# Linear-attention denominators by DMA transpose and VectorE instead of a TensorE matmul

## The chip, the cores and the metric

The kernel runs on one core of one Trainium2 chip. The metric is the device time of one execution in microseconds (us). A core has five engines that run their own instruction streams side by side and meet at semaphores: TensorE (PE in the profile; its weight loads are listed as PEld), VectorE (DVE), ScalarE (ACT), GpSimd (POOL) and SyncE (SP), which here only issues DMAs. SP issues them one after the other: where the next DMA waits for a semaphore, all that are behind it in the program wait too.

## The reference

Two linear-attention blocks A and B with weights of their own run on the same x (2048 rows, 640 columns), and a sigmoid gate mixes them. Each has 32 heads of 20 columns.

```python
def block(x, wqkv, wo):                          # A and B alike
    q, k, v = split(x @ wqkv)                    # 32 heads of 20 columns
    phi = lambda t: where(t > 0, t + 1, exp(t)) + 1e-6
    pq, pk = phi(q), phi(k)
    kv  = einsum("bhsd,bhse->bhde", pk, v)
    z   = einsum("bhsd->bhd", pk)                # column sums of pk
    num = einsum("bhqd,bhde->bhqe", pq, kv)
    den = einsum("bhqd,bhd->bhq", pq, z) + 1e-6  # one number for each row of x and head
    return (num / den) @ wo

g = sigmoid((x * gate_w).sum(-1))
out = g * block_A(x) + (1 - g) * block_B(x)
```

The change concerns `den`, its inverse, and how the inverse, times the gate, comes to the values of pq that it scales.

## The kernel before

The 2048 rows are 16 tiles of 128 (`t`) or four blocks of 512 (`b`). The 640 columns of q and k are five groups `g` of 128: group g holds the columns g, g+5, g+10 and so on, so a partition p of any group belongs to head p // 4, and each head has four neighbouring partitions, 4h to 4h+3.

The order of the work on PE is the order in which the program text makes it. On the other engines a planner in the kernel (`Sched`) lays every instruction into a timeline by an assumed cost and a priority; the program that results is fixed, and each engine runs its instructions in that order. The stages on PE are:

- K for A and B (L513, L514), from the start to 48 us; exp on ACT, min and add on DVE, results in PKA and PKB.
- G of A (L644, L645), pk transposed times x, with a column of ones that yields z; between its matmuls the query units (`q_unit`, L767): five matmuls fill one PSUM bank, ACT takes exp (L784) and relu (L791) of it, DVE puts them together as pq (L794, L802), in EX, PKA or GSA.
- G of B with the rest of the query units, and between them for A: kv (`kv_unit`, L685, masked by DVE at L700), the denominators (`den`, L850), and WP = kv times wo (`wp_unit`, L721, copied by ACT at L735 and moved into place by DMA).
- The outputs of A for 13 tiles (`o_part`, L937, kept by ACT), and between them the denominators, kv and WP of B; then the outputs of B for these tiles (`o_rest`, added by DVE at L974), then three tiles with A and B in one accumulation.

The results of G leave PSUM by ACT (L653) into WKW, and a DMA transpose of 128x640 turns them into GSA and GSB.

The denominators go as follows. `t_sum` (L827, L830) multiplies pq of each group by its z, a scalar for each partition, and adds the five groups in float32; the last addition writes bf16 into TSH, 128 x 512 for each block. `den` multiplies a 128x32 mask of ones (the columns of CST from 24 on) with TSH: four matmuls put the four blocks into 32 partitions each of one PSUM bank, so that partition 32b+h holds the denominators of head h in block b. ACT adds 1e-6 (L869), DVE inverts (L879, eight RECIPROCALs of 128x128 for A and B together) and multiplies by the gate (L888). The gate, known for each row of x as a column, had been turned by DVE (L610), written to DRAM by four DMAs and read back by eight that spread it over 32 partitions. Nine DMAs copy each row of the product to the four partitions of its head (FXT: for A over WVA, for B over XN), and DVE multiplies pq by it in halves of 256 rows (`pqs`, L915). `o_mm` (L937) waits for the half it reads and for WP.

Of the kernel before, what the change touches and what calls it, by code (L numbers as in the profile page):

```python
# [28 lines left out]
def _consts():  # L29
    p = np.arange(128)[:, None]  # L30
    bd = (p // 20 == np.arange(24)[None, :] // 4).astype(np.float32)
    zm = (p // 4 == np.arange(H)[None, :]).astype(np.float32)
    return _bf16_bits(np.concatenate([bd, zm], axis=1))


CW = 24 + H
XS_W = 672
KB_W = 648

# [219 lines left out]
def body(nc, A_x, A_wqkv, A_wo, B_x, B_wqkv, B_wo, gate_w, out, log=None):  # L259
# [53 lines left out]
    TSF = [TSB[:, 1024 * b : 1024 * b + 1024].bitcast(f32) for b in range(NB)]  # L313
    TSH = sb("TSH", [128, NB, 512], bf)
    ZC = sb("ZC", [128, 2 * NC], f32)
    DTT = sb("DTT", [128, 512], f32)
    RCT = sb("RCT", [128, 512], f32)
    FF = {X: sb("FF" + X, [128, 512], bf) for X in XS}
    GB = {X: sb("GB" + X, [128, 512], f32) for X in XS}
    CST = sb("CST", [128, CW], bf)  # L320
    GW5 = sb("GW5", [NC, 128], bf)
    GE = sb("GE", [128, NT], f32)
    GG = sb("GG", [128, 2, NT], f32)
    GT = sb("GT", [128, 32], f32)
    ONE = sb("ONE", [128, 128], bf)
    SCR = sb("SCR", [128, 1], f32)
    EPSC = sb("EPSC", [128, 1], f32)
    PS = nc.alloc_psum_tensor("ps", [128, 8, 512], f32)

    GD = nc.dram_tensor("ggd", [2, S], f32, kind="Internal").ap()  # L330

    IDN = sb("IDN", [128, 128], bf)
    BDM = CST[0:GR, 0:24]
    ZMK = CST[:, 24:CW]

    sch = Sched({"ps": 8, "ek": NEK, "eq": NEQ, "os": NOS})
    op = sch.op
# [257 lines left out]

    LOW = 10**6

    bge2, bgg, bgg2, bgt = Buf("ge2"), Buf("gg"), Buf("gg2"), Buf("gt")
    op("DVE", lambda e: e.tensor_scalar(GG[:, 1, :], GE[:, :], 1.0, None, op0=ALU.add), 150.0, ins=bge, outs=[bge2], prio=LOW + 50, name="ge1")
    op("DVE", lambda e: e.reciprocal(GG[:, 0, :], GG[:, 1, :]), 250.0, ins=[bge2], outs=[bgg], prio=LOW + 51, name="gr")  # L600
    op(
# [5 lines left out]
        prio=LOW + 52,  # L607
        name="gm",
    )
    op("DVE", lambda e: e.transpose(GT[:, :], GG[:, :, :].rearrange("p a b -> p (a b)")), 200.0, ins=[bgg, bgg2], outs=[bgt], prio=LOW + 53, name="gt")  # L610
    bgd = []
    gflat = GD.rearrange("a (t q j) -> (a t) q j", q=4, j=32)
    for q in range(4):
        b = Buf("gd%d" % q)
        bgd.append(b)
        dma("SP", "gd%d" % q, gflat[:, q, :], GT[32 * q : 32 * q + 32, :], 4096, ins=[bgt], outs=[b])
    bgb = {X: [] for X in XS}
    for i, X in enumerate(XS):
        for j in range(NB):
            b = Buf("gb")  # L620
            bgb[X].append(b)
            dma(
                "SP",
                "gb%s%d" % (X, j),
                GB[X][32 * j : 32 * j + 32, :],
                GD[i, 512 * j : 512 * j + 512].partition_broadcast(32),
                65536,
                ins=bgd,
                outs=[b],
            )  # L630


    bgs = {}
    bz = {}
# [37 lines left out]
        )  # L672

    bkvl = {X: [] for X in XS}

    def kv_unit(X):
        gv = GS[X][:, :, :].rearrange("p c (g m) -> p c g m", g=NC)
        for us in ((0, 1, 2, 3), (4, 5)):
            ps = Buf("kv", "ps")

            def fn(e, us=us, ps=ps):
                for i, u in enumerate(us):
                    lo = GR * u if u < 5 else D - GR
                    for c in range(NC):
                        r = e.matmul(  # L685
                            PS[0:GR, ps.slot, GR * i : GR * i + GR],
                            WV[X][:, c, lo : lo + GR],
                            gv[:, c, :, lo // 5 : lo // 5 + 24],
                            start=(c == 0),
                            stop=(c == NC - 1),  # L690
                        )
                return r

            op("PE", fn, 5 * len(us) * mm_cost(GR), ins=[bwv[X]] + [bgs[X, g] for g in range(NC)], outs=[ps], name="kv" + X)
            b = Buf("kvl")
            bkvl[X].append(b)
            n = len(us)
            op(
                "DVE",
                lambda e, us=us, ps=ps, n=n: e.tensor_tensor(  # L700
                    out=KVL[X][:, us[0] : us[0] + n, :].rearrange("p u (m g) -> p u g m", g=NC),
                    in0=PS[0:GR, ps.slot, 0 : GR * n].rearrange("p (u g m) -> p u g m", u=n, g=NC),
                    in1=BDM.unsqueeze(1).unsqueeze(1).to_broadcast([GR, n, NC, 24]),
                    op=ALU.mult,
                ),
                dve1(GR * n),
                ins=[ps, bcst],
                outs=[b],
                prio=-1,
                name="kvm",  # L710
            )
# [99 lines left out]
    def scale_now(X, b, h):  # L811
        pqs_op[X, b, h].prio = len(sch.ops)

    prev_rc = [[], []]

    bts, last_ts = {}, {}

    def t_sum(X, b):
# [3 lines left out]
        for g in range(NC):  # L822
# [1 line left out]
            src = PQ[X, b][:, g, :]  # L824
            n = Buf("ts")
            if g == 0:
                f = lambda e, z=z, src=src: e.tensor_scalar(TSF[b], src, z, None, op0=ALU.mult)  # L827
            else:
                dst = TSF[b] if g < NC - 1 else TSH[:, b, :]
                f = lambda e, z=z, src=src, dst=dst: e.scalar_tensor_tensor(dst, src, z, TSF[b], op0=ALU.mult, op1=ALU.add)  # L830
# [1 line left out]
            if b in last_ts and g == 0:  # L832
                after = [last_ts[b]]
            if g == NC - 1 and X == "B":
                after = [den_op["A"]]
            last = op(
                "DVE", f, dve1(512), ins=[bz[X, g], bpq[X, b, g]] + prev, outs=[n], after=after, prio=LOW + 20 * i + b, name="ts"
            )
# [1 line left out]
        last_ts[b] = last  # L840
        bts[X, b] = n

    den_op = {}

    def den(X):
        ps = Buf("den", "ps")

        def fn(e):
            for j in range(NB):
                r = e.matmul(  # L850
                    PS[32 * j : 32 * j + 32, ps.slot, :],
                    ZMK,
                    TSH[:, j, :],
                    start=True,
                    stop=True,
                    tile_position=(0, 32 * j),
                )
            return r

        den_op[X] = op("PE", fn, mm_cost(512) + 200, ins=[bcst] + [bts[X, b] for b in range(NB)], outs=[ps], name="den" + X)  # L860
        dops = [sch.ops[-1]]
        halves = []
        for h in range(2):
            q = slice(256 * h, 256 * h + 256)
            b1, b2, b3 = Buf("dt"), Buf("rc"), Buf("ff")
            halves.append(b3)
            op(
                "ACT",
                lambda e, q=q: e.activation(DTT[:, q], PS[:, ps.slot, q], ACT.Identity, bias=EPSC[:, 0:1], scale=1.0),  # L869
                act_cost(256),  # L870
                ins=[ps, beps],
                outs=[b1],
                after=prev_rc[h][0:1],
                name="dt",
            )
            for k in (256 * h, 256 * h + 128):
                rc = op(
                    "DVE",
                    lambda e, k=k: e.reciprocal(RCT[:, k : k + 128], DTT[:, k : k + 128]),  # L879
                    1010.0,  # L880
                    ins=[b1],
                    outs=[b2],
                    after=prev_rc[h][1:2],
                    name="rc",
                )
            ff = op(
                "DVE",
                lambda e, q=q: e.tensor_tensor(out=FF[X][:, q], in0=RCT[:, q], in1=GB[X][:, q], op=ALU.mult),  # L888
                dve1(256),
                ins=[b2] + bgb[X],  # L890
                outs=[b3],
                name="ff",
            )
            prev_rc[h] = [rc, ff]
        for b in range(NB):
            parts = ((0,), (1,)) if X == "B" and b == 0 else ((0, 1),)
            for hs in parts:
                bx = Buf("fx")
                q = slice(256 * hs[0], 256 * hs[-1] + 256)
                dma(  # L900
                    "SP",
                    "fx%s%d%d" % (X, b, hs[0]),
                    FXT[X][:, b, q],
                    FF[X][32 * b : 32 * b + 32, q].unsqueeze(1).to_broadcast([H, 4, 256 * len(hs)]),
                    65536 * len(hs),
                    ins=[halves[h] for h in hs],
                    outs=[bx],
                    issue=650.0,
                )
                for h in hs:  # L910
                    bs = Buf("pqs")
                    bfx[X, b, h] = bs
                    pqs_op[X, b, h] = op(
                        "DVE",
                        lambda e, b=b, h=h: e.tensor_tensor(  # L915
                            out=PQ[X, b][:, :, 256 * h : 256 * h + 256],
                            in0=PQ[X, b][:, :, 256 * h : 256 * h + 256],
                            in1=FXT[X][:, b, 256 * h : 256 * h + 256].unsqueeze(1).to_broadcast([128, NC, 256]),
                            op=ALU.mult,
                        ),  # L920
                        150 + 1280 * 0.52,
                        ins=[bx] + [bpq[X, b, g] for g in range(NC)],
                        outs=[bs],
                        after=dops,
                        name="pqs",
                    )


    def o_mm(X, t, ps, lo, hi, first="A", last="B"):
# [185 lines left out]
```

## Time and profile before

| | |
|---|---|
| median of 5 runs | 189.73 us (189.42 to 190.11) |
| the profiled execution | 189.42 us |
| its span, first to last instruction | 188.0 us |
| VectorE busy | 128.7 us |
| ScalarE busy | 95.9 us |
| denominator matmuls L850 | 8, each recorded with 390 ns, at 105.1 us (A) and 142.7 us (B) |
| DTT activations L869 | 4, median 476 ns |
| RECIPROCAL L879 | 8, mean 920 ns |
| gate multiplication L888 | 4 of 128x256, 425 to 494 ns |
| pqs L915 | 16 of 128x1280, mean about 820 ns |
| copies FFA to WVA and FFB to XN | 9 DMAs, about 2.6 us from issue to landing |
| mean granted TensorE clock | 1.000 |

A busy time is the time in which the engine had an instruction of its own in work. TensorE's matmuls overlap: a 128x512 matmul is recorded with some 380 ns, but in a run of them a new one starts about every 216 ns. So what a matmul costs the engine is read from the distance of the starts. In a group's line, the idle time behind the bar is that of the engine just before these instructions, with what ended it.

### The profile page before, as it was taken

What the parts mean: (1) busy time and instruction counts of PE and PEld (TensorE: products, weight loads), DVE (VectorE), ACT (ScalarE), POOL (GpSimd) and SP (SyncE); (2) the same over time, 40 slices, a digit from 0 to 9 for tenths busy, and PEclk for the clock granted to TensorE, in tenths of its full rate; (3) what the DMA queues carried; (4) which work ended last, traced back from release to release, by engine and by line L of the source; (5) the groups of instructions that cost most, each with busy time, mean ns of one, the idle gap of its engine ahead of it and who ended that gap; (6) DMA issues with size and microseconds to landing.
All of it is one profiled execution on the core that took longest, in us unless ns stands there. A gap on an engine that the chain in (4) does not pass through costs nothing.

```text
span 188.0 us, 3199 instructions
## 1 busy us (share of the span) xinstructions
PE 184.2 (98%) x1250; PEld 108.5 (58%) x1274; DVE 128.7 (68%) x252; ACT 95.9 (51%) x172; POOL 0.6 (0%) x7
## 2 busy tenths in 40 slices
PE   9999999999999999999999999999999999999995
PEld 5555555555556556656557556655666655555552
DVE  3489888878743546578787698888996962765600
ACT  3265556565554454545594777876626595100012
POOL 1000000000000000000000000000000000000000
PEclk9999999999999999999999999999999999999999
DMA  7979999995023101012010005430020054133322
GB/s 222 272 149 162 286 390 364 322 217 118 1 63 86 21 18 35 0 35 38 0 34 0 3 8 140 118 91 5 1 50 19 17 149 123 38 139 106 138 75 70
DMA packets 29469, 19.39 MB, mean 103 GB/s; under 512 B 17390, under 2 KB 29198, under 8 KB 29454
## 3 DMA queue, kind: packets, MB, share of 16 engines
q1 hardware_dynamic: 29012, 18.97, 37.9%
q10 hardware_dynamic: 442, 0.21, 0.4%
q8 instruction: 10, 0.16, 0.4%
q14 instruction: 5, 0.04, 0.1%
HBM read 9.92 MB, written 2.64 MB: 67 GB/s over the span
## 4 chain that ended last, share of the span: by engine, by line
PE 98%; issue 1%; DVE 0%; DVEq 0%
PE ps L937 23%; PE ps L767 23%; PE ps L513 18%; PE ps L644 18%; PE ps L645 5%; PE ps L514 5%; PE ps L685 2%; PE ps L447 1%; PE ps L721 1%; PE ps L460 0%; PE ps L722 0%; PE ps L850 0%; DVE TSB L981 0%; DVE ONE L377 0%; PE ps L494 0%
## 5 line engine op out<-in xcount | busy, mean ns | idle before, releaser
L513 PE MATMUL ps<-WKW,XT 128*128 128x512 bf16 x154 | 43.2, 381 | 0.0
L784 ACT ACTIVATE EK<-ps 128x512 bf16<-128x512 f32 x40 | 23.9, 599 | 31.3 <-PE ps L767 30.1
L514 PE MATMUL ps<-WKW,XT 128*128 128x128 bf16 (+1 forms) x160 | 35.2, 220 | 0.3
L546 ACT ACTIVATE EK<-ps 128x640 bf16<-128x640 f32 x32 | 22.3, 703 | 11.3 <-PE ps L514 5.0
L513 PEld LDWEIGHTS ps<-WKW,XT 128*128 128x128 bf16 x160 | 15.7, 98 | 18.8 <-DVE XT L475 0.4
L767 PE MATMUL ps<-XT,WQA 128*128 128x512 bf16 x96 | 24.1, 379 | 0.2
L767 PE MATMUL ps<-XT,WQB 128*128 128x512 bf16 x98 | 23.6, 379 | 0.1
L794 DVE TENSOR_SCALAR EK<-EK 128x512 bf16<-128x512 bf16 x40 | 11.6, 291 | 17.4 <-ACT EK L784 17.3
L644 PE MATMUL ps<-XN,PKA 128*128 128x512 bf16 x78 | 23.1, 379 | 0.0
L644 PE MATMUL ps<-XN,PKB 128*128 128x512 bf16 x76 | 22.8, 379 | 0.0
L645 PE MATMUL ps<-XN,PKB 128*128 128x129 bf16 x80 | 17.6, 220 | 0.2
L645 PE MATMUL ps<-XN,PKA 128*128 128x129 bf16 x80 | 17.6, 220 | 0.1
L937 PE MATMUL ps<-WPA,EX 128*128 128x512 bf16 (+1 forms) x118 | 17.0, 298 | 0.1
L937 PE MATMUL ps<-WPB,PKA 128*128 128x128 bf16 (+1 forms) x117 | 16.1, 297 | 0.2
L767 PEld LDWEIGHTS ps<-XT,WQB 128*128 128x128 bf16 x100 | 10.9, 118 | 8.5 <-issue 0.2
L514 PEld LDWEIGHTS ps<-WKW,XT 128*128 128x128 bf16 x160 | 15.7, 98 | 0.0
L767 PEld LDWEIGHTS ps<-XT,WQA 128*128 128x128 bf16 x100 | 10.7, 117 | 8.1
L549 DVE TENSOR_SCALAR EK<-EK 128x640 bf16<-128x640 bf16 x32 | 10.4, 325 | 7.1 <-ACT EK L546 6.8
L644 PEld LDWEIGHTS ps<-XN,PKA 128*128 128x128 bf16 x80 | 9.4, 117 | 7.9
L644 PEld LDWEIGHTS ps<-XN,PKB 128*128 128x128 bf16 x80 | 9.4, 117 | 7.8
L983 ACT ACTIVATE TSB<-ps 128x640 bf16<-128x640 f32 (+1 forms) x3 | 2.0, 668 | 23.2 <-PE ps L937 23.2
L557 DVE SCALAR_TENSOR_TENSOR PKA<-ps,EK 128x640 bf16<-128x640 f32 x16 | 13.2, 825 | 0.6
(79 smaller groups left out, 233.9 us busy)
## 6 DMA issues: line engine op xcount, KB each, us to landing
out_dram<-TSB SPq DMA_DIRECT2D x15, 160.0 KB, 1.8
XN<-in_A_x_dram SPq DMA_DIRECT2D x1, 2240.0 KB, 9.0
WKW<-in_A_wqkv_dram SPq DMA_DIRECT2D x5, 160.0 KB, 3.5
WKW<-in_B_wqkv_dram SPq DMA_DIRECT2D x5, 160.0 KB, 3.6
WQA<-in_A_wqkv_dram SPq DMA_DIRECT2D x1, 800.0 KB, 10.6
WQB<-in_B_wqkv_dram SPq DMA_DIRECT2D x1, 800.0 KB, 13.3
WVA<-in_A_wqkv_dram SPq DMA_DIRECT2D x1, 800.0 KB, 12.7
WVB<-in_B_wqkv_dram SPq DMA_DIRECT2D x1, 800.0 KB, 14.1
```

Source lines behind the costliest of these rows:

```text
L513: e.matmul(a[:, 0:512], l, WK[X][:, c, 0:512], start=(c == 0), stop=(c == NC - 1))
L514: return e.matmul(a[:, 512:w], l, WK[X][:, c, 512:w], start=(c == 0), stop=(c == NC - 1))
L546: op("ACT", lambda e: e.activation(EK[:, ek.slot, :], psw(ps, D), ACT.Exp), act_cost(D), ins=[ps] + first, outs=[ek], name="ke")
L549: lambda e: e.tensor_scalar(EK[:, ek.slot, :], EK[:, ek.slot, :], 1.0, EPS, op0=ALU.min, op1=ALU.add),
L557: lambda e: e.scalar_tensor_tensor(PKt[X][:, t, :], psw(ps, D), 0.0, EK[:, ek.slot, :], op0=ALU.max, op1=ALU.add),
L644: e.matmul(a[:, 0:512], l, XN[:, t, 0:512], start=(t == 0), stop=(t == NT - 1))
L645: return e.matmul(a[:, 512 : D + 1], l, XN[:, t, 512 : D + 1], start=(t == 0), stop=(t == NT - 1))
L685: r = e.matmul(PS[0:GR, ps.slot, GR * i : GR * i + GR], WV[X][:, c, lo : lo + GR], gv[:, c, :, lo // 5 : lo // 5 + 24], start=(c == 0), st ...
L767: r = e.matmul(PS[:, ps.slot, :], WQ[X][:, c, g::5], XT[:, c, 512 * b : 512 * b + 512], start=(c == 0), stop=(c == NC - 1),)
L784: lambda e: e.activation(EQ[:, eq.slot, :], PS[:, ps.slot, :], ACT.Exp),
L794: lambda e: e.tensor_scalar(EQ[:, eq.slot, :], EQ[:, eq.slot, :], 1.0, EPS, op0=ALU.min, op1=ALU.add),
L937: r = e.matmul(a[:, l0 - lo : h0 - lo], PQ[X, b][:, g, 128 * (t % 4) : 128 * (t % 4) + 128], WP[X][:, g, l0:h0], start=(X == first and g = ...
```

## The change

`den` no longer uses PE or ACT. For each block of 512 rows:

1. a DMA transpose turns TSH (128 x 512, partitions are 4h+j) into TTR, four 128x128 tiles in which the partition is the row of x and the columns are 4h+j;
2. DVE sums the four columns of each head (TENSOR_REDUCE, 128x512 to 128x128 float32);
3. DVE inverts them (RECIPROCAL, 128x128, in place);
4. DVE multiplies by the gate, which is now a scalar per partition and tile, and writes every value four times (128x512 bf16, FF);
5. a second DMA transpose turns FF back into FXT.

The 1e-6 is now put in at the first step of `t_sum`, a quarter in each of the four partitions of a head. The gate's turn by DVE and its twelve DMAs through DRAM are dropped, with the mask and the tiles DTT, RCT, GB and GT. For A the second transpose has to wait for the kv matmuls of A, since FXT of A lies over WVA; the last addition of `t_sum` of B waits for the first transpose of the same block of A in place of the matmul. `pqs` and `o_mm` are as before.

```diff
-CW = 24 + H
+CW = 24
...
-    op("DVE", lambda e: e.transpose(GT[:, :], ...), 200.0, ins=[bgg, bgg2], outs=[bgt], prio=LOW + 53, name="gt")
-    for q in range(4):
-        dma("SP", "gd%d" % q, gflat[:, q, :], GT[32 * q : 32 * q + 32, :], 4096, ins=[bgt], outs=[b])
-    for i, X in enumerate(XS):
-        for j in range(NB):
-            dma("SP", "gb%s%d" % (X, j), GB[X][32 * j : 32 * j + 32, :],
-                GD[i, 512 * j : 512 * j + 512].partition_broadcast(32), 65536, ins=bgd, outs=[b])
...
     def t_sum(X, b):
-                f = lambda e, z=z, src=src: e.tensor_scalar(TSF[b], src, z, None, op0=ALU.mult)
+                f = lambda e, z=z, src=src: e.tensor_scalar(TSF[b], src, z, EPS / 4, op0=ALU.mult, op1=ALU.add)
...
             if g == NC - 1 and X == "B":
-                after = [den_op["A"]]
+                after = [tt_op[b]]
...
     def den(X):
-        ps = Buf("den", "ps")
-            for j in range(NB):
-                r = e.matmul(PS[32 * j : 32 * j + 32, ps.slot, :], ZMK, TSH[:, j, :],
-                             start=True, stop=True, tile_position=(0, 32 * j))
-        for h in range(2):
-            op("ACT", ... e.activation(DTT[:, q], PS[:, ps.slot, q], ACT.Identity, bias=EPSC[:, 0:1], scale=1.0), ...)
-            for k in (256 * h, 256 * h + 128):
-                rc = op("DVE", ... e.reciprocal(RCT[:, k : k + 128], DTT[:, k : k + 128]), 1010.0, ...)
-            ff = op("DVE", ... e.tensor_tensor(out=FF[X][:, q], in0=RCT[:, q], in1=GB[X][:, q], op=ALU.mult), ...)
-        for b in range(NB):
-            dma("SP", "fx...", FXT[X][:, b, q], FF[X][32 * b : 32 * b + 32, q].unsqueeze(1).to_broadcast([H, 4, ...]), ...)
+        for b in range(NB):
+            tt_op[b] = dma("SP", "tt%s%d" % (X, b), TTR[:, b, :, :], TSH[:, b, :], 131072, ins=[bts[X, b]], outs=[b1],
+                after=[red_op[b]] if b in red_op else (), issue=900.0, transpose=True)
+            red_op[b] = op("DVE", lambda e, b=b: e.tensor_reduce(out=DNT[:, b, :],
+                    in_=TTR[:, b, :, :].rearrange("p t (h j) -> p (t h) j", j=4), op=ALU.add, axis=AX.X),
+                dve1(512), ins=[b1], outs=[b2], after=[ff_op[b]] if b in ff_op else (), name="rd")
+            op("DVE", lambda e, b=b: e.reciprocal(DNT[:, b, :], DNT[:, b, :]), 1010.0, ins=[b2], outs=[b3], name="rc")
+            ff_op[b] = op("DVE", lambda e, b=b: e.tensor_tensor(
+                    out=FF[:, b, :].rearrange("p (t h j) -> p t h j", t=4, j=4),
+                    in0=DNT[:, b, :].rearrange("p (t h) -> p t h", t=4).unsqueeze(3).to_broadcast([128, 4, H, 4]),
+                    in1=GG[:, i, 4 * b : 4 * b + 4].unsqueeze(2).unsqueeze(3).to_broadcast([128, 4, H, 4]), op=ALU.mult),
+                dve1(512), ins=[b3, bgg, bgg2], outs=[b4], after=[ft_op[b]] if b in ft_op else (), name="ff")
+            ft_op[b] = dma("SP", "fx%s%d" % (X, b), FXT[X][:, b, :].rearrange("p (t s) -> p t s", t=4), FF[:, b, :],
+                131072, ins=[b4], outs=[bx], after=kv_op[X], issue=900.0, transpose=True)
...
-                        after=dops,
                         name="pqs",
```

## The prediction

> **What bounds the kernel now.** I read the page's busy times and chain of waits first, to see which engine sets the end.
>
> ```profile
> PE 184.2 (98%) x1250; PEld 108.5 (58%) x1274; DVE 128.7 (68%) x252; ACT 95.9 (51%) x172; POOL 0.6 (0%) x7
> PE 98%; issue 1%; DVE 0%; DVEq 0%
> ```
>
> The chain that ended last is PE in 98% of the span: no other engine makes it wait. So time is won only by what leaves PE, and lost only by what makes PE wait. Next the timeline of PE around the denominator matmuls (start, duration, line):
>
> ```profile
> 103.91 1.24 PE L767 MATMUL ps<-XT,WQB 128*128 128x512 bf16 x4
> 105.08 0.40 PE L850 MATMUL ps<-TSH,CST 128*32 128x512 bf16 x4
> 105.42 1.27 PE L767 MATMUL ps<-XT,WQB 128*128 128x512 bf16 x5
> ...
> 138.54 4.24 PE L937 MATMUL ps<-WPA,EX 128*128 128x512 bf16 x30
> 142.71 0.40 PE L850 MATMUL ps<-TSH,CST 128*32 128x512 bf16 x4
> 143.04 1.53 PE L937 MATMUL ps<-WPA,EX 128*128 128x512 bf16 x10
> ...
> 160.14 16.25 PE L937 MATMUL ps<-WPB,PKA 128*128 128x128 bf16 x117
> ```
>
> The four matmuls overlap, so the cost is read from starts. The last line is the start of `o_rest(0)`, the first work that needs pq of B scaled. Third, busy time by stage (PE, PEld, DVE, ACT), since all the new work but its DMAs goes to DVE:
>
> ```profile
> 95.00:135.00 40.00, 39.74 (x252) 23.97 (x256) 33.48 (x74) 29.30 (x54) 0.00 (x0) 1.00 0.19 47
> 135.00:143.00 8.00, 7.95 (x61) 4.61 (x60) 7.21 (x12) 2.38 (x5) 0.00 (x0) 1.00 0.21 41
> ```
>
> From 95 to 135 us, where the denominators of A are made, DVE has 40 - 33.5 = 6.5 us idle; until 143 it is nearly full. Fourth, rows of DVE (count, busy us, mean ns) that price the new instructions, and those of the DMA transposes:
>
> ```profile
> L830 DVE SCALAR_TENSOR_TENSOR TSB<-PKA,ZC,TSB 128x512 f32<-128x512 bf16 x12 | 8.8, 749 | 0.2
> L879 DVE RECIPROCAL RCT<-DTT 128x128 f32<-128x128 f32 x8 | 7.0, 920 | 1.4 <-ACT DTT L869 1.4
> L888 DVE TENSOR_TENSOR FFA<-RCT,GBA 128x256 bf16<-128x256 f32 x2 | 0.9, 426 | 0.2
> L700 DVE TENSOR_TENSOR KVLB<-ps,CST 120x480 bf16<-120x480 f32 x1 | 1.5, 1503 | 0.0
> L700 DVE TENSOR_TENSOR KVLB<-ps,CST 120x240 bf16<-120x240 f32 x1 | 0.9, 912 | 0.0
> ```
> ```profile
> L348 SPq DMA_TRANSPOSE GSB<-WKW x5: 1201/1202/1311, 96.7 to 139.5; - x5
> DMA to landing us min/median/max: 2.6/2.6/2.9
> ```
>
> Last the timeline in which the denominators of B are made, where the new chain is longest:
>
> ```profile
> 139.47 1.20 SPq L348 DMA_TRANSPOSE GSB<-WKW  x1
> 139.73 2.08 DVE L830 SCALAR_TENSOR_TENSOR TSH<-PKA,ZC,TSB 128x512 bf16<-128x512 bf16 x3
> ...
> 144.41 1.81 PE L685 MATMUL ps<-GSB,WVB 128*120 128x120 bf16 x30
> 145.71 2.17 DVE L700 TENSOR_TENSOR KVLB<-ps,CST 120x480 bf16<-120x480 f32 x2
> ...
> 147.41 0.38 PE L721 MATMUL ps<-WOB,KVLB 120*120 120x512 bf16 x1
> ```
>
> **PE: the eight matmuls go.** From 103.91 to 105.42 are 1.51 us; the query unit in it needs 1.08 (elsewhere ten of these matmuls start 2.16 us apart), so the denominators of A take 0.43. From 138.54 to 143.04 are 4.50 us; three output units at 1.36 (143.04 to 144.41 is one) are 4.08, so those of B take 0.42. PE's order is otherwise unchanged. Gain: 0.85 us, all on the chain. ACT's four DTT copies (about 1.9 us) go too; ACT mostly waits for PE, so this counts nothing.
>
> **DVE: price of the new instructions.** Before the change no reduction and no broadcast of this kind runs. The reduction reads 512 bf16 values: at least 0.29 us (L794, 512 values, 291 ns) and at most what L700's rate gives: (1503 - 912) / 240 = 2.46 ns for a value, so 0.91 + 272 x 2.46 ns = 1.58 us. L700 writes with gaps and in short rows, which makes it the dearest neighbour. I take L830's 0.75, which works through 512 bf16 values one by one. The gate multiplication writes 512 values from float32: at least 0.43 (L888, half the size), at most the same 1.58. From L888 (256 values, 0.425) and L974 (640 values, 0.825) comes 1.04 ns a value, so 0.69; I take that, since types and contiguous output are L888's. The inversion keeps shape and count (L879). On DVE that is 8 x (0.75 + 0.69) = 11.5 us added, 1.8 (four L888) and 0.2 (the gate's turn) removed.
>
> The multiplication reads each float32 word four times before it goes on. [...] No row here has a repeated word at the inner step.
>
> **Where A's half lies.** It adds 4 x 1.44 - 0.85 = 4.9 us to DVE, mostly in a stage with 6.5 idle. The new program sets its pieces between the query posts in place of the one block that ran from 106.7 to 111.1. What is displaced are sums of `t_sum` for B. After the last query post there are ten additions and, new, one L827 (0.48): the last TSH comes some 0.45 us later. Cover against late query posts: four EK buffers, and ACT, which waits for PE (30.1 us in 28 waits at L784) and nowhere in this stage for DVE. With that cover gone, DVE's lateness would hit PE one for one. The last `pqs` of A ended at 123.3 and PE needs the first at 138.1, so A's chain itself has over 10 us.
>
> **SP.** Removed: 4 + 8 gate DMAs and 9 copies; added: 16 transposes. A transpose of five tiles occupies SP for 1.20 us, one of twenty 4.13 (XT), so four tiles cost about 1.0. Three transposes of A stand before GSB's first; three returns of A (the first behind kv of A on PE) and the fourth transpose stand before GSB's second; the last return stands before four of the six moves of WPA. GSB is wanted at 143.6 and WPA at 138.1, over 10 us after these: that hides them. In B's tail the three last moves of WPB stand behind the second return: FF of that block is ready at 151.0, the last move is issued at about 154.7, now 155.0. No loss.
>
> **B's tail, step by step.** PE is 0.43 earlier before 142.7, 0.85 after. TSH of block 0 is written at 140.48, now 140.9. GSB's last transpose leaves SP by 140.3; TTR is issued at 141.0 and lands 2.6 later, 143.6 (2.6 is the least; XT's median from DRAM, 4.0, is the other end). Reduction until 144.35. Behind it on DVE is the mask of kv (L700), for which PE's matmuls are ready at 145.71 - 0.85 = 144.86: 0.5 us spare. The mask's first half ends at 146.36 and `wp_unit` on PE wants it at 147.41 - 0.85 = 146.56: 0.2 more. So 0.7 us of lateness is covered here, and what exceeds it stalls PE. Mask done 147.03; inversion and gate of block 0 1.61; three blocks at 0.75 + 0.92 + 0.69 = 2.36: 155.7. Only then comes the first `pqs` (0.82): 156.5. `o_rest(0)` stands at 160.14 - 0.85 = 159.3, so 2.75 us are spare. Later halves come every 0.78 us and PE needs one per 2.7. The first L974 is about 0.5 us late; three more output slots in PSUM hide it. Seven new instructions lie between mask and `pqs`: they may be 0.39 us longer each, 1.14 and 1.08, before PE waits.
>
> **Sum.** Span 188.0 - 0.85 + 0 = 187.15; with the 1.42 around it (189.42 - 188.0) 188.57. That execution lies 0.31 below the median of the runs, so the median should be 188.9.
>
> **Rivals.**
>
> 1. Slower: the new DVE instructions run at L700's rate because of short rows of four. For it: L700 itself, and a copy of five single values (L497) that takes 25 ns more than one of one value (L656), 6 ns a row, 0.8 us for 128 rows. Against: L830 and L888 stream at about 1 ns. It decides from about 1.1 us each. With the multiplication alone at 1.58, A's half is 4.9 + 3.6 - 6.5 = 2.0 late and the tail 3.6 - 2.75 = 0.8: 189.73 - 0.85 + 2.8 = 191.7. With both: 11.8 - 6.5 = 5.3 and 7 x 0.86 - 2.75 = 3.3, so 197.5. Chance 0.15.
> 2. The wait for TTR takes the place of the matmul: it lands after 4.0, the mask is 1.4 late, 0.7 over its cover: 189.6, no change. For it: four transposes in a row, which no row of DMAs between SBUF tiles shows. Against: GSB's spread is 2.6 to 2.9. Chance 0.08.
> 3. PE's 0.43 is a gap of its queue that stays (PEld shows 0.41 "issue" ahead of L850): 189.7. Against: other changes between kinds of matmul there show no such gap. Chance 0.05.
>
> **From this to numbers.** The forecast has 0.72, with a range of its own of 188.6 to 189.2. The 8-in-10 range is 188.4 to 190.3: below, 0.85 and the runs' scatter; above, rivals 2 and 3 and a first part of rival 1. A change under 0.2% (0.38 us) is about what a measurement of this kernel cannot tell from none. Faster than 189.35: forecast and a little of rival 2, 0.73. Within: 0.12. Slower than 190.11: rival 1, 0.15.
>
> **What will show it.** Right: L937 starts at once after the third output unit at about 142.2; TENSOR_REDUCE near 0.75 and the gate multiplication near 0.7; PE 98% of the chain; a first `pqs` of B by 157. Wrong: PE idle before `wp_unit` of B (mask late), before `o_rest(0)` (pqs late) or at query units near 105 (DVE behind); a reduction over 1.1 us or TTR landing after 3.3 us.

## The result and the profile after

The changed kernel takes 189.23 us (median of 37 runs, 188.44 to 189.79), the kernel before, run beside it, 189.80 (63 runs, 189.03 to 190.51). The ratio is 0.9967 with a 95% interval of 0.9959 to 0.9976, so it is 0.63 us faster (0.46 to 0.78). Forecast were 0.85 us and a median of 188.9. The measured median lies inside the 8-in-10 range (188.4 to 190.3) and 0.03 us above the narrower range that the prediction gave the forecast itself (188.6 to 189.2).

The busy times of the page and the chain of work that ended last, of the kernel after:

```profile
PE 183.7 (98%) x1242; PEld 108.6 (58%) x1266; DVE 136.0 (72%) x263; ACT 94.5 (50%) x168; POOL 0.6 (0%) x7
PE 94%; DMA 2%; ACT 1%; issue 1%; SPq 0%; DVE 0%; DVEq 0%
```

PE has lost its eight matmuls (1250 to 1242), DVE has 7.3 us more busy time, and PE still is nearly the whole chain. The 2% of DMA is the load of the second slice of K weights at the very start, which was late in this execution; the 1% of ACT lies just ahead of a query unit (131.28 us) whose first matmul is missing from the trace, and PE shows no wait there. So times are best read from one PE landmark to another. The timeline of PE after (start, duration, line): kv of A, kv of B, the first WP matmul of B, and `o_rest(0)`:

```profile
100.69 1.81 PE L659 MATMUL ps<-GSA,WVA 128*120 128x120 bf16 x30
...
144.11 1.81 PE L659 MATMUL ps<-GSB,WVB 128*120 128x120 bf16 x30
...
147.11 0.38 PE L697 MATMUL ps<-WOB,KVLB 120*120 120x512 bf16 x1
...
159.84 16.25 PE L903 MATMUL ps<-WPB,PKA 128*128 128x128 bf16 x117
```

From kv of A to kv of B are 43.4 us; before it was 144.41 - 100.1 = 44.3. This stretch holds both sets of denominator matmuls, and it has become 0.9 us shorter. From kv of B to `o_rest(0)` are 15.7 us as before (160.14 - 144.41): B's new chain delays nothing there. (Both rows of `o_rest(0)` begin with a 128x128 matmul; the 128x512 one ahead of it is missing from both traces. In f5, f6 and f8 below, whose traces hold every matmul, the distance is 15.5, so `o_rest(0)` really starts 0.2 us earlier than the rows say, before and after.) But kv of A itself comes at 100.7 here and came at 100.1 before: the slices of WKW landed 4.0 us after issue (median), 3.5 before. That is why the span of this execution (187.7) is only 0.3 below the 188.0 of before.

The prices of the new instructions on DVE, which were estimates (count, busy us, mean ns):

```profile
L838 DVE TENSOR_REDUCE DNT<-TTR 128x128 f32<-128x512 bf16 x8 | 5.4, 679 | 0.0
L853 DVE TENSOR_TENSOR FF<-DNT,GG 128x512 bf16<-128x512 f32 x8 | 5.5, 688 | 0.2
L850 DVE RECIPROCAL DNT<-DNT 128x128 f32<-128x128 f32 x8 | 7.6, 946 | 0.2
```

Both stream 512 values in 0.68 us, about 1.3 ns a value with the start included. The reduction in groups of four is no dearer than the 749 ns of L830 before, which works through 512 dense values, and the multiplication that reads each denominator four times has the price that was worked out from dense operands (0.69). The transposes of TSH into TTR on SP (shortest, median and longest issue in ns, first and last start; then issue to landing):

```profile
L343 SPq DMA_TRANSPOSE TTR<-TSH x8: 1189/1264/1267, 89.5 to 144.8; - x8
DMA to landing us min/median/max: 2.4/2.5/3.6
```

Seven of the eight landed after 2.4 to 2.5 us. The one of 3.6 is the last block of B, issued at 144.8 and wanted at 153.5. It is over the 3.3 us that the prediction named as a sign of being wrong, at a place where it delays nothing.

And DVE from the last TSH of B to the first `pqs` of B:

```profile
142.58 0.75 DVE L804 SCALAR_TENSOR_TENSOR TSH<-GSA,ZC,TSB 128x512 bf16<-128x512 bf16 x1
143.34 0.69 DVE L838 TENSOR_REDUCE DNT<-TTR 128x128 f32<-128x512 bf16 x1
145.41 2.17 DVE L676 TENSOR_TENSOR KVLB<-ps,CST 120x480 bf16<-120x480 f32 x2 [1.38 <-PE ps L659]
147.33 0.91 DVE L850 RECIPROCAL DNT<-DNT 128x128 f32<-128x128 f32 x1
...
155.20 0.69 DVE L853 TENSOR_TENSOR FF<-DNT,GG 128x512 bf16<-128x512 f32 x1
155.81 3.02 DVE L882 TENSOR_TENSOR PKA<-PKA,XN 128x1280 bf16<-128x1280 bf16 x4
```

The reduction of block 0 is done 1.38 us before the mask of kv has anything to do, so the wait for TTR delays no one. The rest is a block without gaps until 155.81; its first half is ready at about 156.6, and PE starts `o_rest(0)` at about 159.6.

There remains a question of sizes. The stretch between the landmarks gave 0.9 us, the measured gain is 0.63. Part of the difference is not in the span at all: 189.43 - 187.7 = 1.73 us of this execution lie outside it, where it was 189.42 - 188.0 = 1.42 before. That, and the prices of lateness on DVE, are what the experiments are about.

### The profile page after: what moved, and what is told of

Same layout as the page of the kernel before. It is cut to its first block, busy times and chain, and to the rows that moved or that the text cites. A ratio compares the mean times of both kernels' runs of the same rounds, so it can differ in the third digit from the quotient of the medians.

```text
span 187.7 us, 3183 instructions
## 1 busy us (share of the span) xinstructions
PE 183.7 (98%) x1242; PEld 108.6 (58%) x1266; DVE 136.0 (72%) x263; ACT 94.5 (50%) x168; POOL 0.6 (0%) x7
## 4 chain that ended last, share of the span: by engine, by line
PE 94%; DMA 2%; ACT 1%; issue 1%; SPq 0%; DVE 0%; DVEq 0%
PE ps L903 23%; PE ps L743 22%; PE ps L508 18%; PE ps L617 17%; PE ps L509 5%; PE ps L618 5%; DMA WKW<-in_A_wqkv_dram 2%; PE ps L659 2%; PE ps L697 1%; ACT EK L760 1%; ACT GSA L767 1%; SPq L343 0%; PE ps L698 0%; DVE TSB L947 0%; PE ps L489 0%
## 5 line engine op out<-in xcount | busy, mean ns | idle before, releaser
L508 PEld LDWEIGHTS ps<-WKW,XT 128*128 128x128 bf16 x160 | 15.7, 98 | 19.0 <-DMA WKW<-in_A_wqkv_dram 0.5
L903 PE MATMUL ps<-WPA,EX 128*128 128x128 bf16 (+1 forms) x117 | 16.6, 297 | 0.2
L509 PEld LDWEIGHTS ps<-WKW,XT 128*128 128x128 bf16 x160 | 15.7, 98 | 0.0
L552 DVE SCALAR_TENSOR_TENSOR PKB<-ps,EK 128x640 bf16<-128x640 f32 x16 | 13.2, 825 | 0.6
```

The lines of the kernel that those rows point to most:

```text
L508: e.matmul(a[:, 0:512], l, WK[X][:, c, 0:512], start=(c == 0), stop=(c == NC - 1))
L509: return e.matmul(a[:, 512:w], l, WK[X][:, c, 512:w], start=(c == 0), stop=(c == NC - 1))
L552: lambda e: e.scalar_tensor_tensor(PKt[X][:, t, :], psw(ps, D), 0.0, EK[:, ek.slot, :], op0=ALU.max, op1=ALU.add),
L903: r = e.matmul(a[:, l0 - lo : h0 - lo], PQ[X, b][:, g, 128 * (t % 4) : 128 * (t % 4) + 128], WP[X][:, g, l0:h0], start=(X == first and g = ...
```

## Experiments

From the second run on, the experiments are built on copies of both kernels in which every DMA transpose is a plain DMA of as many bytes between the same places, at the same point of SP's program. The values that come out of them are then not the transposed ones, so the denominators, and all that comes after them, are other numbers; the programs of PE, DVE and ACT are the same as those of the two kernels. A plain copy of four tiles occupies SP for about 0.5 us where the transpose takes 1.19 to 1.27, so SP has more room in these copies than in the two kernels. In `dma`:

```diff
-                return e.dma_start(d, src() if callable(src) else src, transpose=transpose)
+                s = src() if callable(src) else src
+                if transpose:
+                    n = s.shape[0] // 128
+                    if n > 1:
+                        s = s.rearrange("(p n) d -> p (n d)", n=n)
+                    s = s.rearrange("p (c z) -> p c z", c=d.shape[1])
+                return e.dma_start(d, s)
```

In the table, the starts of kv of A, kv of B and `o_rest(0)` are of the profiled execution of each; time, span and what lies around the span are medians of all timed runs of the kernel. (For "before" the last three columns are of the 35 runs beside f1 to f4; for the run e8 and the three starts of "before" of one execution. The spans are on record to 0.1 us.) In the traces of f5 to f8 every matmul is recorded; in the others 24 are missing, the first of `o_rest(0)` among them, so that column is 0.2 us late there.

| kernel | kv A | kv B | B - A | `o_rest(0)` | time | span | around |
|---|---|---|---|---|---|---|---|
| before | 100.1 | 144.4 | 44.3 | 160.1 | 189.74 | 188.4 | 1.36 |
| e8 before, again | 101.1 | 145.4 | 44.3 | 161.2 | 190.41 | 189.0 | 1.41 |
| after | 100.7 | 144.1 | 43.4 | 159.8 | 189.23 | 187.5 | 1.73 |
| f1 before, plain copies | 100.2 | 144.5 | 44.3 | 160.2 | 189.64 | 188.3 | 1.38 |
| f2 after, plain copies | 100.2 | 143.6 | 43.4 | 159.4 | 188.99 | 187.25 | 1.73 |
| f3 f2 + dead matmuls | 100.6 | 144.9 | 44.3 | 160.6 | 190.06 | 188.35 | 1.70 |
| f4 f2, wide constants | 100.7 | 144.1 | 43.4 | 159.8 | 189.08 | 187.35 | 1.70 |
| f5 f2, late constants | 100.5 | 143.9 | 43.4 | 159.4 | 189.23 | 187.5 | 1.72 |
| f6 f2, B's gate twice | 100.4 | 143.9 | 43.4 | 159.4 | 189.07 | 187.45 | 1.60 |
| f7 f2, B's sums and gate twice | 100.1 | 143.5 | 43.4 | 160.6 | 191.19 | 189.8 | 1.39 |
| f8 f2, A's sums and gate twice | 100.6 | 145.9 | 45.3 | 161.4 | 191.85 | 190.5 | 1.35 |
| g1 f1 + 11 memsets | 100.3 | 144.6 | 44.3 | 160.4 | 189.75 | 188.35 | 1.40 |
| g2 f2 + 8 memsets | 100.6 | 144.0 | 43.4 | 159.8 | 189.83 | 188.45 | 1.37 |
| g3 f2 + 24 memsets | 100.8 | 144.2 | 43.4 | 160.0 | 189.16 | 187.8 | 1.36 |

### e8: the kernel before once more

No edit; a second profile of the same program. In the expectation, "144.3 us" from kv of A to kv of B is a slip for 44.3.

> The kernel before once more, for a second profile of its start. Theory 1 (the start varies): kv of A between 100.0 and 100.7, kv of A to kv of B 144.3 us. Theory 2 (its start is always the early one): kv of A at 100.1 within 0.1.

Kv of A came at 101.1 instead of 100.1, and the whole program about 1 us later; the 44.3 us between the landmarks stayed. The first matmuls of K show two parts of this, in the first profile and then in e8:

```profile
3.54 0.63 PE L513 MATMUL ps<-WKW,XT 128*128 128x512 bf16 x1
4.42 0.38 PE L513 MATMUL ps<-WKW,XT 128*128 128x512 bf16 x1
4.75 0.39 PE L513 MATMUL ps<-WKW,XT 128*128 128x512 bf16 x1
5.08 0.39 PE L513 MATMUL ps<-WKW,XT 128*128 128x512 bf16 x1
```
```profile
3.92 0.61 PE L513 MATMUL ps<-WKW,XT 128*128 128x512 bf16 x1
4.96 0.63 PE L513 MATMUL ps<-WKW,XT 128*128 128x512 bf16 x1
5.50 0.63 PE L513 MATMUL ps<-WKW,XT 128*128 128x512 bf16 x1
6.03 0.45 PE L513 MATMUL ps<-WKW,XT 128*128 128x512 bf16 x1
```

The first slice of weights landed 3.4 us after issue in e8 and 2.7 before, and the first matmul is 0.4 later. The next ones then start 0.53 us apart instead of 0.33. What slows them is not shown. So the start of one and the same program moves by 1 us from one execution to the next, and a comparison of two profiled spans can be wrong by as much; the 35 spans of before beside f1 to f4 run from 187.7 to 189.2. Landmarks and medians are what the rest goes by.

### f1 and f2: both kernels with plain copies

> The kernel before, with all its DMA transposes (7 of x, 10 of G) as plain copies of the same bytes to the same places in the same order; so what is computed from x and G is not turned. It is the base for what follows. All engine programs are otherwise the same. Expected: within 1 us of before, ratio 0.995 to 1.005; kv of A to kv of B 44.3 us as in the profile of before (100.10 to 144.41).

> The changed kernel with its transposes (7 of x, 10 of G, 16 new) as plain copies of the same bytes. Theory 1 (eight matmuls give 0.85 to 0.89; everything new is hidden; the 0.63 measured lacks a part by the scatter of the start): 0.85 us less than f1 between kv of A and the end, in the median 0.6 to 0.9 less. Theory 2 (the new program starts later every time, by its constants of 48 bytes a row or otherwise): 0.4 to 0.65 less than f1, and the first K matmuls later than in f1 by 0.2 or more.

f1 against before: 1.0001 (0.9986 to 1.0016). f2 against before: 0.9965 (0.9948 to 0.9981), so it has the gain of the changed kernel (0.9967). That the new DMAs transpose costs nothing that can be measured here, and the pair can stand for the two kernels, except for the time that SP is occupied.

### f3: the matmuls put back

f2 with the four matmuls of each half at their old places, on tiles that are there anyway, with the constants 56 columns wide again; their result is not used.

```diff
     def den(X):
         i = XS.index(X)
+        dead = Buf("dead", "ps")
+        def dfn(e):
+            for j in range(NB):
+                r = e.matmul(PS[32 * j : 32 * j + 32, dead.slot, :], CST[:, 24:CW],
+                             XT[:, 0, 512 * j : 512 * j + 512], start=True, stop=True, tile_position=(0, 32 * j))
+            return r
+        op("PE", dfn, 0.0, ins=[bcst] + bxt[2:], outs=[dead], name="dead")
```

> f2 with eight 32-column matmuls back on TensorE at the two old places (on x transposed; constants 56 wide as before the change); nothing reads what they write, and the new chain on VectorE and the DMAs stay. Theory 1: 0.85 us slower than f2 (0.7 to 1.0), kv of A to kv of B 44.3 us again, and as fast as f1 within 0.3, since the new chain costs nothing. Rival 3 of the prediction (a gap of TensorE's queue that stays without them): under 0.4 us slower than f2.

190.06 us, 1.07 more than f2; the stretch between the landmarks is 44.3 again. The timeline of PE in f3:

```profile
104.40 1.24 PE L750 MATMUL ps<-XT,WQB 128*128 128x512 bf16 x4
105.57 0.40 PE L833 MATMUL ps<-XT,CST 128*32 128x512 bf16 x4
105.90 1.27 PE L750 MATMUL ps<-XT,WQB 128*128 128x512 bf16 x5
...
143.19 0.40 PE L833 MATMUL ps<-XT,CST 128*32 128x512 bf16 x4
```

So the eight matmuls are worth 0.9 us on PE, all of it on the path, and they are the whole gain in the span: f3's span (188.35) is that of before (188.4). But f3 is not back at 189.74. Its time is 0.3 us longer than before (ratio 1.0014, 1.0000 to 1.0029) with the same span, as 1.70 us lie around it. The term that eats a part of the gain comes with the change, and not with the matmuls.

### f4 and f5: the constants

The change also makes the first DMA of ACT, the constants, smaller (24 columns of CST instead of 56). f4 loads the wide constants again, f5 loads them last.

```diff
-    return _bf16_bits(bd)
+    zm = (p // 4 == np.arange(H)[None, :]).astype(np.float32)
+    return _bf16_bits(np.concatenate([bd, zm], axis=1))
-CW = 24
+CW = 24 + H
```
```diff
-    dma("ACT", "cst", CST[:, :], cap[:, :], 128 * CW * 2, outs=[bcst])
...
+    dma("SP", "cst", CST[:, :], cap[:, :], 128 * CW * 2, outs=[bcst])
     loading.clear()
```

> f2 with constants 56 columns wide (112 bytes a row in place of 48), loaded at the same place; the added columns are not used. Theory 2 in its form 'rows of 48 bytes at the head of the queue slow the first loads': 0.2 to 0.5 us faster than f2. Theory 1: as f2 within 0.15 us.

> f2 with the load of the constants taken from the head of ScalarE's queue and issued by SP after all other loads; they are wanted at 102 us. If that load stands in the way of the first slices of K weights: 0.1 to 0.5 us faster than f2, first K matmuls earlier by as much. If the weights alone set the start: as f2 within 0.15 us.

f4: 0.9962 (0.9947 to 0.9976); f5: 0.9979 (0.9964 to 0.9993). Neither differs from f2 by more than the intervals hold, the stretch is 43.4 in both, and 1.70 and 1.72 us lie around their spans. Width and place of this load are not the missing part.

### f6 and f7: lateness in B's tail

In f6 each gate multiplication of B is issued twice, first into TTR's columns, which are used up by then; in f7 each reduction of B as well, first into FF.

```diff
-                lambda e, b=b: e.tensor_tensor(
-                    out=FF[:, b, :].rearrange(...),
+                lambda e, b=b: [
+                    e.tensor_tensor(
+                        out=d.rearrange(...),
...
+                    for d in ([TTR[:, b, :, :].rearrange("p t c -> p (t c)")] if X == "B" else []) + [FF[:, b, :]]
+                ][-1],
```

> f2, and each of the four gate multiplications of B runs twice (the first time into a tile that is free); the order of all engines else unchanged. Adds 4 x 0.61 to 0.69 = 2.4 to 2.8 us between the mask of kv and the first scaling of B. In the profile of the changed kernel that scaling ends at 156.6 and TensorE starts the outputs of B at about 159.6: 3.0 us spare. Theory 1 (cover of 3 us): as f2 within 0.15 us, first scaling done at about 159.2. Rival (the tail already is on the chain): 2.4 us slower.

> f6 with the four reductions of B doubled too. The reduction of block 0 lies before the mask of kv, where VectorE waits 1.4 us; so seven more instructions of 0.61 to 0.70, 4.3 to 4.9 us, lie before the first scaling. Theory 1: 3.0 is covered, TensorE waits for the rest before the outputs of B: 1.3 to 1.9 us slower than f2. Rival (more cover further on): as f2.

f6 is 189.07, as f2 (188.99): four more instructions before the first `pqs` are covered, and `o_rest(0)` starts 15.5 us after kv of B, as in f5. f7 is 191.19, 2.2 more than f2. PE's timeline shows the wait that was asked for, and below it stand the first `pqs` of B in f2 and in f7:

```profile
157.68 1.52 PE L915 MATMUL ps<-WPA,PKA 128*128 128x512 bf16 x10
160.61 2.60 PE L915 MATMUL ps<-WPB,PKA 128*128 128x512 bf16 x18 [1.41 <-DVE PKA L894]
```
```profile
155.34 4.49 DVE L888 TENSOR_TENSOR PKA<-PKA,XN 128x1280 bf16<-128x1280 bf16 x6
```
```profile
159.40 4.49 DVE L894 TENSOR_TENSOR PKA<-PKA,XN 128x1280 bf16<-128x1280 bf16 x6
```

PE stood still for 1.41 us before `o_rest(0)`. Counted by starts, it lost 1.6: from kv of B to `o_rest(0)` are 17.1 us in f7 and 15.5 in f6. The doubled instructions start 0.60 us apart, and seven of them lie between the mask and the first `pqs`, which is 4.2 us later counted from kv of B. 4.2 - 1.6 gives a cover of 2.6 us in the changed kernel; 2.75 were forecast, from a row of `o_rest(0)` that begins 0.2 us late. The 2.4 us of f6 fit in. The rest of f7's 2.2 us has nothing to do with this wait; see g2.

### f8: lateness in A's stage

The same doubling for A (both instructions, `X == "A"`).

> f2, and the four reductions and four gate multiplications of A run twice: 4.9 to 5.5 us more on VectorE between 94 and 117 us. In the profile of the changed kernel VectorE is idle 3.8 us from 95 to 135 and 0.2 until 144, and then waits 1.4 for kv of B; the mask has 0.2 spare. The prediction counts lateness over that as TensorE's loss one for one: 5.2 - 5.6 is none, so 0 to 0.8 us slower than f2, lost at the query units near 105 us or at WP of B. Rival (query units have no cover in EK and PSUM): TensorE waits there for most of it, 3 us or more slower.

191.85 us, 2.86 more than f2, far above the 0 to 0.8 that the forecast's way of counting cover had been taken to give. DVE's busy time by stage, f2:

```profile
95.00:135.00 40.00, 39.74 (x250) 24.27 (x254) 36.21 (x81) 28.82 (x53) 0.00 (x0) 1.00 0.18 50
135.00:145.00 10.00, 9.95 (x90) 6.47 (x89) 8.29 (x14) 3.52 (x5) 0.00 (x0) 1.00 0.30 85
```

and f8:

```profile
95.00:135.00 40.00, 38.67 (x241) 22.77 (x240) 38.69 (x84) 27.06 (x50) 0.00 (x0) 1.00 0.18 50
135.00:145.00 10.00, 10.00 (x74) 6.04 (x73) 9.58 (x19) 4.38 (x8) 0.00 (x0) 1.00 0.24 65
```

(The columns are PE, PEld, DVE and ACT.) Eight instructions that start 0.60 us apart add 4.8 us to DVE. In f2 it has 3.8 us idle from 95 to 135, in f8 1.3, while PE drops from 39.74 to 38.67. One place where it waits, in f8:

```profile
105.67 2.35 PE L749 MATMUL ps<-XT,WQB 128*128 128x512 bf16 x10 [1.12 <-DVE KVLA L682]
```

The mask of kv of A (L682) stands in DVE's program behind the doubled instructions of two blocks, four of them, or 2.4 us; in f2 DVE waits 0.62 us for its input. It is late, keeps its PSUM bank, and the next query unit waits for the bank: 1.3 us, counted by starts. Another 0.5 is lost by 124 us: ACT waits 1.75 us for a late query post of DVE (until 120.85), and PE then waits for ACT's copy of WP. Between the landmarks 1.9 us are lost (45.3 against 43.4). As with f7, 0.8 us of the total belong to g2's effect; compared with g2, which has the same number of instructions on DVE, f8 costs 2.0 us.

### g1, g2, g3: the time around the span

What lies around the span is narrow in every kernel, and the two groups do not overlap: 1.32 to 1.44 us in 35 runs of before, 1.68 to 1.80 in the 38 of after, 1.69 to 1.78 in f2. f6 lies between them (1.47 to 1.68). f7 and f8 have the lower value again, though at their end other things are late. What f6, f7 and f8 change against f2 is DVE's program (267, 271 and 271 recorded instructions for 263) and a few waits for the doubled instructions. So instructions that do nothing were added there, in a stretch in which DVE is idle at the start:

```diff
     op("DVE", lambda e: e.memset(ONE[:, :], 1.0), 120.0, outs=[bone], name="one")
+    op("DVE", lambda e: [e.memset(PAD[:, k : k + 1], 0.0) for k in range(N)][-1], 0.0, outs=[Buf("pad")], name="pad")
```

> The kernel before with plain copies for its transposes, and at its start, where VectorE is idle until the first transposed tile of x (0.34 to 2.4 us), 11 further memsets of one column each into a scratch tile: VectorE then runs 263 instructions as the changed kernel does, and nothing else differs from the same kernel without them (189.64 us; 188.3 in the span, 1.375 around it by the medians of 12 runs). Theory: what lies around the span follows the place that VectorE's instructions have reached by the end, so it goes to about 1.72 and the time to 190.0, with the span at 188.3. Rival: it belongs to the new transfers, the shorter programs of TensorE and ScalarE or to the removed matmuls: 1.37 and 189.65.

> The changed kernel with plain copies and 8 such memsets: VectorE runs 271 instructions, as in the two runs in which eight of its instructions were doubled (1.35 and 1.385 us around the span, the last cast 0.46 us after the last matmul where it is 0.11 otherwise, the last output 2.3 us from issue to landing where it is 1.6). Against 188.99 us, with 187.25 in the span and 1.735 around it. Theory: the same tail without any work being late: span 188.2 to 188.3, 1.37 around it, 189.6 to 189.7 in all. Rival (the tail of those two runs came from their late work): 188.99, 187.25 and 1.73.

> The changed kernel with plain copies and 24 such memsets (287 instructions on VectorE). If the event at the end is tied to one place in VectorE's program, 24 instructions put it into the stretch before the last output, where VectorE waits 7 us for TensorE: span 187.25, 1.37 around it, 188.6 in all, the fastest of these kernels. If the number of VectorE's instructions has nothing to do with it: 188.99 and 1.73. If it comes again every few instructions, something between 188.6 and 189.7.

g2 is the clear one: 189.83 us, 0.84 more than f2, by eight memsets of one column, which run 0.28 us after the start, with the landmarks 0.4 later in its profile and the stretch at 43.4. (g1 to g3 ran on another chip than f1 to f8; the kernel before took 189.63 beside them and 189.74 beside f1 to f4. f7 and f8 show the same end on the chip of f2.) The end of f2's timeline (last matmuls, last cast, last output's issue):

```profile
184.68 0.44 PE L909 MATMUL ps<-WPB,GSA 128*128 128x128 bf16 x5
185.22 0.29 DVE L953 CAST TSB<-ps 128x128 bf16<-128x128 f32 x1 [7.32 <-PE ps L909]
185.55 0.37 ACTq L349 DMA_DIRECT2D out_dram<-TSB  x1
```

and of g2's:

```profile
185.09 0.44 PE L911 MATMUL ps<-WPB,GSA 128*128 128x128 bf16 x5
185.99 0.29 DVE L955 CAST TSB<-ps 128x128 bf16<-128x128 f32 x1 [7.67 <-PE ps L911]
186.31 0.37 ACTq L350 DMA_DIRECT2D out_dram<-TSB  x1
```

The cast starts 0.10 us after the last matmul's end in f2 and 0.46 in g2. The last output then takes longer as well (last column, us from issue to landing), f2 and then g2:

```profile
out_dram<-TSB ACTq DMA_DIRECT2D x1, 32.0 KB, 1.6
```
```profile
out_dram<-TSB ACTq DMA_DIRECT2D x1, 32.0 KB, 2.4
```

0.36 + 0.8 in the span, less 0.36 around it, makes the 0.8. f7 ends in the same way (its cast at 187.03 after matmuls to 186.57), and so does f8. So with g2 as their measure, f7's lateness costs 1.36 us and f8's 2.0; between landmarks it is 1.6 and 1.9.

g3 has the 1.36 around its span that was expected, but 0.55 more in the span, and is no faster than f2 (189.16): in its profile kv of A started at 100.8, 0.6 later than in f2's. PE waited for no weights there: its matmuls of K started 0.5 us apart until 5.8 us, as in e8, and in f2 0.28 apart from 4.66 on. Whether the 24 memsets have to do with that was not tried. g1 has 1.40, the rival's number: eleven instructions more on DVE in the kernel before do not bring 1.73. So the number of DVE's instructions alone does not set it; in the changed program instructions added on DVE move it, wherever they stood (g2, f7, f8). What it is that sits at the end of the program stays open.

## Why the prediction was right, and where it was short

- **PE's gain, 0.43 + 0.42.** Right: 0.9 between the landmarks in both pairs, and put back by f3. Rival 3 (a gap of PE's queue that stays) is out.
- **Prices on DVE.** Reduction 0.75 forecast, 0.679 measured; gate 0.69 and 0.688; inversion 0.92 and 0.946. Rival 1 (L700's 2.46 ns a value in these instructions too) is out: they take 1.3, the start included. Why L700 is dear was not tested.
- **The repeated word.** No row of before has a float32 word that is read four times, so the 0.69 of the gate multiplication was the author's estimate from dense operands. The 688 ns show no extra cost for this pattern: from L888 (256 values of two dense operands, 426 ns) to L853 (512 values, 688 ns) a value takes 1.02 ns, where L888 and L974 (640 values, 825 ns) gave 1.04.
- **SP.** A transpose of four tiles occupies SP for 1.19 to 1.27 us, not the 1.0 worked out from the sizes of 5 and 20 tiles. Sixteen of them make 3 to 4 us more than counted; no landmark moved in the changed kernel itself, so the named cover (GSB and WPA over 10 us ahead) took it.
- **TTR's landing.** 2.5 us for 2.6 (one of 3.6, where it does no harm); rival 2 is out. The reduction was done 1.38 us before the mask's input, where 0.5 had been counted.
- **B's tail.** Forecast: mask ready at 144.86 and the first `pqs` from 155.7. Measured, less the 0.6 us by which this execution started late: 144.8 and 155.2. The 2.75 us of cover were 2.6 by f7.
- **A's half.** "4.9 in 6.5 idle" held, no landmark moved. From 95 to 135 DVE's busy time grew by 2.7 us (33.5 to 36.2); the rest of the half lies outside or displaced other work, and 3.8 us of idle were left. But the prediction's rule for the stage (lateness beyond the idle hits PE one for one) is too kind: it gives 4.8 - 3.8 = 1.0 for f8, and 1.9 were lost between the landmarks. It counts idle time that comes after the instruction that is late. In a fixed order such idle does not help: the mask of A in the middle of the stage already held up PE. The forecast was not put to this test, since nothing in A's half was late.
- **The sum.** Here is the step that was mis-sized: "with the 1.42 around it". The prediction carried over what lies around the span as a constant of the measurement. No row backed that, as the prediction had one kernel only. It measured 1.73 in the changed kernel. 188.0 - 0.85 + 1.73 + 0.31 = 189.2, which is the measured median. The forecast's 0.85 is in the span (188.4 to 187.5 by the medians), and 0.37 us (1.73 - 1.36) are given back outside it. f3, f4, f5 and f2 show that neither the matmuls, nor the constants, nor the transposing makes this part, and g2, f7 and f8 that eight more instructions on DVE move it; the mechanism is not shown.

No version here beats the changed kernel: f2, f4, f5, f6 and g3 lie within each other's intervals, and they don't compute the reference.

## What to carry to other kernels

This kernel, bound by one engine, gained in its span what left this engine, to 0.1 us. That holds as long as no new wait reaches the engine, so check each at the place where it lands: read the cover there, ahead of the first waiting instruction, not as an engine's idle time over a stage. Judge gains of less than 1 us between landmarks inside the program, since starts scatter by 1 us, and compare time less span separately: it is a part of the time that an edit can change. When an experiment adds instructions, run the same number of idle ones beside it as a control.

## What was not expected of the hardware

- Eight VectorE memsets of one column, in an idle stretch at the start, cost 0.84 us at the end of the program: the last cast starts 0.36 us later after its input, and the last output lands after 2.4 us instead of 1.6. Four doubled instructions (f6) or 24 memsets (g3) do not do this.
- A transpose of four 128x128 tiles occupies SP as long (1.19 to 1.27 us) as one of five (1.20).
- VectorE reduces 512 bf16 values in groups of four in 679 ns and multiplies with each float32 word repeated four times in 688 ns: about what dense operands of that size take here (749 ns for L830, 0.69 us from L888 and L974).
- The same program starts its kv of A at 100.1 or 101.1 us. Part of it is when its first weights land; the larger part is that its first matmuls start 0.53 us apart instead of 0.33 for longer, at a granted clock that the records give as 1.00.
